# B's keys and values in 32 KB runs, and four heads finished together, in a two-cache attention decode kernel

## The chip, the cores and the metric

The kernel runs on one core of a Trainium2 chip. The metric is the device time of one execution in microseconds (us). A "fast" run is an undisturbed one. Engines: PE multiplies matrices (PEld is its loading of weights), DVE is the vector engine, ACT the scalar engine, POOL does next to nothing here, SP issues the DMAs.

## The reference

Two independent attention decode steps for one token, their outputs side by side. A attends to all 16384 keys of each of 32 heads, B only to the last 4096 keys of each of 32 heads.

```python
def _A_ref(x, k_cache, v_cache, wq, wo):       # x [1,1,512], caches [1,32,16384,128]
    q = (x @ wq).reshape(1, 1, 32, 128).transpose(0, 2, 1, 3)
    # ... (k, v are the caches themselves: rep is 1)
    scores = jnp.einsum("bhqd,bhkd->bhqk", q, k) * (128 ** -0.5)
    p = _softmax(scores, axis=-1)
    o = jnp.einsum("bhqk,bhkd->bhqd", p, v)
    return o.transpose(0, 2, 1, 3).reshape(1, 1, 4096) @ wo
# _B_ref: the same with k_cache[:, :, Sk - W:, :] and v_cache[:, :, Sk - W:, :], W = 4096
return jnp.concatenate([a, b], axis=-1)        # [1,1,1024], bfloat16
```

Every key and value is used once. The kernel has to read 352.3 MB.

## The kernel before

A *unit* is one head of A or four heads of B: 128 partitions x 128 keys of keys (4 MB) and the same of values. Key tiles and value tiles have two buffers each. A *chunk* is 64 keys on each partition, so a unit has two chunks. After every four A heads comes one B unit; a B unit is also the last of all.

For each chunk DVE multiplies the keys by the query (a tile `prod`), adds the two halves of the head dimension (`half`), PE sums on with an identity matrix (`red`), DVE ends the sum (`sc`), ACT takes the exponential (`p`), and PE multiplies `p` by the values into an accumulator: for every four keys on a partition a matmul with 4 stationary columns, on one of four column tiles (rows 0, 32, 64, 96).

How B lies in memory is the point of the change. Before, each B head covers all 128 partitions with 32 keys each, so a partition's piece of a head is 32 x 128 x 2 bytes = 8 KB. The four heads lie one behind the other in the tile, so a chunk needs two heads:

```python
def _load_kv(nc, cx, unit, which, cut_last=1):
    # ... (tile of 128 partitions x 128 keys x 128, view of the cache)
    L = st.W // P                                  # A: 128 keys a partition, B: 32
    for i, h in enumerate(unit.heads):
        src = view[h].rearrange("(p l) d -> p l d", p=P)
        cuts = cut_last if i == n - 1 else 1
        w = L // cuts
        for c in range(cuts):
            cx.o(nc.sync.dma_start(
                out=t[:, i * L + c * w : i * L + (c + 1) * w, :],
                in_=src[:, c * w : (c + 1) * w, :],
            ))

def _mult(nc, cx, ch):                             # one multiply for each head in the chunk
    for k0, n, st, h, _, _ in ch.pieces:
        q = st.qall[:, h * DH : (h + 1) * DH]
        cx.o(nc.vector.tensor_tensor(
            out=ch.prod[:, k0 : k0 + n, :],
            in0=ch.unit.kt[:, ch.k0 + k0 : ch.k0 + k0 + n, :],
            in1=q.rearrange("p (o d) -> p o d", o=1).broadcast_to([P, n, DH]),
            op=ALU.mult,
        ))
```

Each head of A and B has its own accumulator and is finished alone: copy, fp32 fold to one row, division, output product.

```python
        cx.o(nc.tensor.matmul(                     # in _pv
            acc[r : r + 4, :],
            lhsT=ch.p[:, k : k + 4],
            rhs=ch.unit.vt[:, ch.k0 + k : ch.k0 + k + 4, :],
            start=(first and t < 4), stop=(last and t >= T - 4)))
    # ...
def _fin_fold(nc, cx, st, heads):
    # ... (sums of the exponentials into column DH)
        for e in range(4):
            cx.o(nc.tensor.matmul(
                f_ps[0:1, x, 0:DH],
                lhsT=cx.sel[:, e : e + 1],
                rhs=acc_sb[:, e * DH : (e + 1) * DH],
                start=False, stop=(e == 3), skip_group_check=True))
```

Loads are issued by SP in a fixed order (keys of unit i, then values of unit i-1) as buffers come free. At the end the last chunks go through without a further multiply:

```python
    _softmax(nc, cx, prev)
    waiting.append(prev)
    for ch in waiting:
        fin_pe()
        fin_dve()
        pv(ch)
    while fins:
        fin_pe()
        fin_dve()
```

The softmax here doesn't subtract the row's maximum and nothing guards it: scores larger than these inputs give would overflow.

## Time and profile before

839.10 us (median of 4 runs, 838.87 to 839.16). The profiled execution has a span of 837.5 us.

The page of the kernel before: span, busy time of the engines, the rate in 40 equal slices of the span, and packets.

```profile
span 837.5 us, 7159 instructions
PE 446.3 (53%) x3007; PEld 175.5 (21%) x3008; DVE 585.5 (70%) x331; ACT 98.6 (12%) x339; POOL 0.8 (0%) x8
...
GB/s 384 443 425 425 417 434 432 431 437 425 417 437 431 423 429 422 436 430 422 437 426 431 424 423 435 426 437 428 425 420 435 436 428 424 416 440 428 427 422 183
DMA packets 21508, 352.79 MB, mean 421 GB/s; under 512 B 2530, under 2 KB 2532, under 8 KB 4836
```

No engine is near full. After the first slice the rate is steady near 430 GB/s, with slices of 416 to 422, until the last one. Groups of instructions of the kernel before (busy us, mean ns of one, then the idle time before them and what ended most of it):

```profile
L146 DVE TENSOR_TENSOR prod<-kt,qallA 128x8192 bf16<-128x8192 bf16 x64 | 283.2, 4425 | 216.3 <-DMA kt<-in_A_k_cache_dram 216.2
...
L146 DVE TENSOR_TENSOR prod<-kt,qallB 128x4096 bf16<-128x4096 bf16 x32 | 72.3, 2289 | 1.7 <-DMA kt<-in_B_k_cache_dram 1.1
L235 PE MATMUL f_ps<-acc_sb,sel 128*1 128x128 f32 x512 | 64.4, 272 | 16.2 <-ACT acc_sb L220 16.2
```

DVE waits 216.2 us for keys of A but only 1.1 us for keys of B. The stretches of the kernel before (window, length, busy us of PE, PEld, DVE, ACT, POOL, then granted PE clock (1.00 is full), share of the DMA engines, GB/s):

```profile
300.00:400.00 100.00, 52.26 (x363) 20.37 (x362) 69.09 (x40) 10.90 (x40) 0.00 (x0) 0.74 1.01 429
...
828.00:830.00 2.00, 2.00 (x26) 0.93 (x23) 0.16 (x1) 1.22 (x4) 0.00 (x0) 1.00 0.02 6
```

In the middle the DMA engines are saturated (share 1.01). From 828 us on they have next to nothing left to do (0.02). The last packet of the values ends at 828.3 us. Their landing is counted here, and in every run below, from the moment at which the load's semaphore is complete in the trace: 828.75 us.

| what | before |
|---|---|
| time, median | 839.10 us |
| DMA share, 100 to 800 us | 1.01, 428 to 429 GB/s |
| packets of 32 KB / of 8 KB | 8320 of 1219 ns / 8064 of 314 ns (mean durations of the DMA records) |
| DVE, PE, ACT busy | 70%, 53%, 12% |
| last values landed, span's end | 828.75 us, 837.5 us |

What does the end hang on? The chain of waits of the kernel before from 762 us on (start, length, what):

```profile
762.20 27.05 DMA kt<-in_A_k_cache_dram
...
789.35 0.06 DVE prod L146
...
818.54 3.57 PE red L171 x8
...
835.00 0.57 ACT rowB L289
```

The last DMA on this chain is the keys of the last *A* head, at 789.3 us. After it the chain runs over DVE and PE to the end. The end is thus a chain of computation over four chunks; the landing of the last values is not on it. But it is close by. PE's timeline of the kernel before at that place:

```profile
828.80 0.62 PE L209 MATMUL acc_101<-vt,p_sb 128*4 128x512 bf16 x5
829.25 1.03 PE L278 MATMUL outA<-wo_t,oc 128*1 128x512 bf16 x4
```

No wait stands before these matmuls. The first of them that needs the last values starts at 829.04 us by the records, 0.3 us after the landing: the two paths to the end differ by no more than that.

### The profile page before, as it was taken

The numbers are of one execution on the slowest core, as the hardware profiler recorded it, in microseconds if no ns is written. First come the engines' busy times: TensorE is split into PE (matmuls) and PEld (weight loads), VectorE is DVE, ScalarE is ACT, GpSimd is POOL, SyncE is SP. The second block draws the span as 40 slices with busy tenths as digits, with TensorE's granted clock in tenths as the row PEclk, the third lists the DMA queues.
The fourth block names the chain that finished last, engine by engine and source line by source line (L and its number), as shares of the span: only waits on it lengthen the run. The fifth ranks groups of instructions, "written<-read, shape, count | busy, mean of one in ns | idle before, by whom it ended". The sixth has DMA issues, their size and how long they took to land.

```text
span 837.5 us, 7159 instructions
## 1 busy us (share of the span) xinstructions
PE 446.3 (53%) x3007; PEld 175.5 (21%) x3008; DVE 585.5 (70%) x331; ACT 98.6 (12%) x339; POOL 0.8 (0%) x8
## 2 busy tenths in 40 slices
PE   3456635555365543655555643456556545355567
PEld 1122212212122211221122211222122112121123
DVE  1892936779577793677867685666947779377791
ACT  2002101001011010100111000111011001010012
POOL 0000000000000000000000000000000000000000
PEclk9578777777787686876778777787687787777678
DMA  9999999999999999999999999999999999999994
GB/s 384 443 425 425 417 434 432 431 437 425 417 437 431 423 429 422 436 430 422 437 426 431 424 423 435 426 437 428 425 420 435 436 428 424 416 440 428 427 422 183
DMA packets 21508, 352.79 MB, mean 421 GB/s; under 512 B 2530, under 2 KB 2532, under 8 KB 4836
## 3 DMA queue, kind: packets, MB, share of 16 engines
q1 hardware_dynamic: 21188, 352.33, 98.7%
q8 instruction: 23, 0.38, 0.2%
q14 instruction: 9, 0.07, 0.0%
q10 hardware_dynamic: 288, 0.00, 0.0%
HBM read 352.32 MB, written 0.00 MB: 421 GB/s over the span
## 4 chain that ended last, share of the span: by engine, by line
DMA 66%; DVE 21%; issue 9%; PE 3%; ACT 1%; SPq 0%; DVEq 0%; ACTq 0%
DMA kt<-in_A_k_cache_dram 53%; DVE prod L146 13%; DMA kt<-in_B_k_cache_dram 10%; DVE half L158 6%; DMA wq_t<-in_B_wq_dram 3%; DVE sc L183 2%; PE q_ps L101 1%; PE f_ps L235 1%; ACT qallB L108 0%; PE red L171 0%; PE acc_101 L209 0%; DVE recip L247 0%; SPq L136 0%; PE outB L278 0%; PE oc_ps L261 0%
## 5 line engine op out<-in xcount | busy, mean ns | idle before, releaser
L146 DVE TENSOR_TENSOR prod<-kt,qallA 128x8192 bf16<-128x8192 bf16 x64 | 283.2, 4425 | 216.3 <-DMA kt<-in_A_k_cache_dram 216.2
L171 PE MATMUL red<-half,ident 128*128 128x512 bf16 x640 | 236.1, 535 | 286.8 <-DVE half L158 286.8
L158 DVE TENSOR_TENSOR half<-prod 128x4096 bf16<-128x4096 bf16 x80 | 182.4, 2280 | 0.0
L171 PEld LDWEIGHTS <-ident 128*128 128x128 bf16 x640 | 78.0, 123 | 404.8 <-issue 376.8
L209 PE MATMUL acc_101<-vt,p_sb 128*4 128x512 bf16 x640 | 58.1, 485 | 59.9 <-DMA vt<-in_A_v_cache_dram 59.9
L146 DVE TENSOR_TENSOR prod<-kt,qallB 128x4096 bf16<-128x4096 bf16 x32 | 72.3, 2289 | 1.7 <-DMA kt<-in_B_k_cache_dram 1.1
L235 PE MATMUL f_ps<-acc_sb,sel 128*1 128x128 f32 x512 | 64.4, 272 | 16.2 <-ACT acc_sb L220 16.2
L187 ACT ACTIVATE p_sb<-sc 128x64 bf16<-128x64 f32 (+1 forms) x96 | 23.5, 245 | 355.3 <-DVE sc L183 355.3
L209 PEld LDWEIGHTS <-p_sb 128*4 128x4 bf16 x1280 | 27.8, 91 | 147.4 <-issue 137.0
L183 DVE TENSOR_REDUCE sc<-red 128x64 f32<-128x512 f32 x80 | 54.6, 683 | 3.7 <-PE red L171 3.7
L209 PE MATMUL acc_103<-vt,p_sb 128*4 128x512 bf16 x640 | 53.1, 448 | 6.0 <-DMA vt<-in_A_v_cache_dram 6.0
L235 PEld LDWEIGHTS f_ps<-acc_sb,sel 128*1 128x1 f32 x512 | 38.2, 83 | 29.2 <-ACT acc_sb L220 18.7
L220 ACT COPY acc_sb<-acc_103 128x512 f32<-128x512 f32 x32 | 18.7, 586 | 140.0 <-PE acc_103 L209 83.1
L220 ACT COPY acc_sb<-acc_101 128x512 f32<-128x512 f32 x32 | 18.8, 588 | 127.6 <-PE acc_101 L209 86.6
L250 ACT ACTIVATE orow<-f_ps,recip 1x128 bf16<-1x128 f32 x64 | 21.2, 354 | 86.4 <-DVE recip L247 86.4
L187 ACT ACTIVATION_READ_ACCUMULATOR p_sb<-sc 128x1 f32 x96 | 18.0, 188 | 0.0
L101 PE MATMUL q_ps<-wq_t,xbA 128*128 128x512 bf16 x32 | 9.3, 462 | 13.2 <-DMA wq_t<-in_A_wq_dram 13.2
L261 PEld LDWEIGHTS <-orow 1*32 1x32 bf16 x256 | 10.0, 110 | 27.7 <-issue 21.4
L261 PE MATMUL oc_ps<-one,orow 1*32 1x1 bf16 x256 | 14.1, 171 | 0.7 <-ACT orow L250 0.7
L229 PE MATMUL f_ps<-ones_col,cs 128*1 128x1 f32 x192 | 14.1, 165 | 0.0
L229 PEld LDWEIGHTS f_ps<-ones_col,cs 128*1 128x1 f32 x192 | 11.5, 85 | 11.7 <-issue 4.5
L247 DVE RECIPROCAL recip<-f_ps 1x1 f32<-1x1 f32 (+1 forms) x48 | 7.2, 150 | 8.2 <-PE f_ps L235 8.2
(25 smaller groups left out, 54.4 us busy)
## 6 DMA issues: line engine op xcount, KB each, us to landing
kt<-in_A_k_cache_dram SPq DMA_DIRECT2D x32, 4096.0 KB, 27.3
vt<-in_A_v_cache_dram SPq DMA_DIRECT2D x31, 4096.0 KB, 31.7
kt<-in_B_k_cache_dram SPq DMA_DIRECT2D x32, 1024.0 KB, 24.0
vt<-in_B_v_cache_dram SPq DMA_DIRECT2D x31, 1024.0 KB, 28.2
wq_t<-in_A_wq_dram SPq DMA_DIRECT2D x1, 4096.0 KB, 12.3
wq_t<-in_B_wq_dram SPq DMA_DIRECT2D x1, 4096.0 KB, 24.1
wo_t<-in_A_wo_dram SPq DMA_DIRECT2D x4, 1024.0 KB, 29.2
wo_t<-in_B_wo_dram SPq DMA_DIRECT2D x4, 1024.0 KB, 30.5
```

Source lines behind the costliest of these rows:

```text
L101: cx.o(nc.tensor.matmul(q_ps[:, :], lhsT=st.xb[:, c, :], rhs=st.wq_t[:, c, j * 512 : (j + 1) * 512], start=(c == 0), stop=(c == KC - 1),))
L146: cx.o(nc.vector.tensor_tensor(out=ch.prod[:, k0 : k0 + n, :], in0=ch.unit.kt[:, ch.k0 + k0 : ch.k0 + k0 + n, :], in1=q.rearrange("p (o d) ...
L158: cx.o(nc.vector.tensor_tensor(out=ch.half[:, :, :], in0=ch.prod[:, :, 0 : DH // 2], in1=ch.prod[:, :, DH // 2 : DH], op=ALU.add,))
L171: cx.o(nc.tensor.matmul(ch.red[:, :, :], lhsT=cx.ident[:, :], rhs=ch.half[:, :, b * W : (b + 1) * W], start=(b == 0), stop=(b == nb - 1),))
L183: cx.o(nc.vector.tensor_reduce(out=sc[:, :], in_=ch.red[:, :, :], axis=AX.X, op=ALU.add))
L187: cx.o(nc.scalar.activation(out=ch.p[:, k0 : k0 + n], in_=sc[:, k0 : k0 + n], func=ACT.Exp, scale=SCALE, accum_out=ch.cs[:, i : i + 1],))
L209: cx.o(nc.tensor.matmul(acc[r : r + 4, :], lhsT=ch.p[:, k : k + 4], rhs=ch.unit.vt[:, ch.k0 + k : ch.k0 + k + 4, :], start=(first and t < ...
L220: cx.o(nc.scalar.copy(st.acc_sb[h][:, :], acc[:, :]))
L229: cx.o(nc.tensor.matmul(f_ps[0:1, x, DH : DH + 1], lhsT=col, rhs=cx.ones_col[:, 0:1], start=(x == 0 and i == 0), stop=(i == len(cs) - 1), ...
L235: cx.o(nc.tensor.matmul(f_ps[0:1, x, 0:DH], lhsT=cx.sel[:, e : e + 1], rhs=acc_sb[:, e * DH : (e + 1) * DH], start=False, stop=(e == 3), s ...
L250: cx.o(nc.scalar.activation(out=orow[:, :], in_=f_ps[0:1, x, 0:DH], func=ACT.Copy, scale=recip[0:1, x : x + 1]))
L261: cx.o(nc.tensor.matmul(st.oc_ps[32 * hp : 32 * hp + 32, j : j + 1], lhsT=orow_j[:, j, :], rhs=cx.one[0:1, 0:1], start=True, stop=True,))
```

## The change

The intent: B's loads in long runs like A's, and far fewer small instructions to finish heads.

- B's head g of a unit goes on the partitions g, g+4, g+8, ...: 32 partitions with 128 keys each, 32 KB a partition. A chunk then holds keys of all four heads, and one multiply serves them: partition p of `qallB` holds the query of head p%4.
- Four heads share one accumulator, 16 rows to a column tile. `p` has zeros in the columns of the other heads. For A the tiles are zeroed once; for B each chunk has four exponentials with a bias of 0 or -1000 (`off`), which makes zeros on the other heads' partitions.
- Sums, fold, division and transposes are done for four heads at once.
- At the end: the last values come as a half and two quarters of the keys, four DMAs each; the last accumulator copy and the output row are split between ACT and DVE.

```diff
-def _load_kv(nc, cx, unit, which, cut_last=1):
+def _load_kv(nc, cx, unit, which, cuts=(2 * U,)):
...
-    L = st.W // P
     n = len(unit.heads)
-    for i, h in enumerate(unit.heads):
-        src = view[h].rearrange("(p l) d -> p l d", p=P)
-        cuts = cut_last if i == n - 1 else 1
-        w = L // cuts
-        for c in range(cuts):
-            cx.o(nc.sync.dma_start(
-                out=t[:, i * L + c * w : i * L + (c + 1) * w, :],
-                in_=src[:, c * w : (c + 1) * w, :],
-            ))
+    k = 0
+    for w in cuts:
+        for g, h in enumerate(unit.heads):
+            src = view[h].rearrange("(p l) d -> p l d", p=P // n)
+            cx.o(nc.sync.dma_start(out=t[g:P:n, k : k + w, :], in_=src[:, k : k + w, :]))
+        k += w
...
 def _softmax(nc, cx, ch):
...
+    for h in u.heads:
+        g = h % G
         cx.o(nc.scalar.activation(
-            out=ch.p[:, k0 : k0 + n],
-            in_=sc[:, k0 : k0 + n],
+            out=ch.p[:, :, g, :],
+            in_=sc[:, :].rearrange("p (t e) -> p t e", e=4),
             func=ACT.Exp,
             scale=SCALE,
-            accum_out=ch.cs[:, i : i + 1],
+            bias=0.0 if len(u.heads) == 1 else cx.off[:, g : g + 1],
+            accum_out=gr.cs[:, ch.i, g : g + 1],
         ))
...
         cx.o(nc.tensor.matmul(
-            acc[r : r + 4, :],
-            lhsT=ch.p[:, k : k + 4],
-            rhs=ch.unit.vt[:, ch.k0 + k : ch.k0 + k + 4, :],
+            gr.acc[r : r + 4 * G, :],
+            lhsT=ch.p[:, t, :, :],
+            rhs=u.vt[:, k : k + 4, :],
...
     if last:
-        st.acc_sb[h] = cx.accs_pool.tile([P, 4 * DH], F32, tag="accs", name="acc_sb")
-        cx.o(nc.scalar.copy(st.acc_sb[h][:, :], acc[:, :]))
+        final = gr.i == gr.st.H // G - 1 and gr.st.name == "B"
+        gr.acc_sb = []
+        for x in range(2):
+            t = cx.accs_pool.tile([P, 2 * DH], F32, tag=f"accs{x}", name="acc_sb")
+            copy = nc.vector.tensor_copy if final and x == 1 else nc.scalar.copy
+            cx.o(copy(t[:, :], gr.acc[:, x * 2 * DH : (x + 1) * 2 * DH]))
...
+    for e in range(4):
+        cx.o(nc.tensor.matmul(
+            gr.f_ps[:, 0:DH],
+            lhsT=cx.sel[:, e, :],
+            rhs=gr.acc_sb[e // 2][:, (e % 2) * DH : (e % 2 + 1) * DH],
+            start=False, stop=(e == 3), skip_group_check=True,
+        ))
...
-        cx.o(nc.scalar.copy(row[0:1, :], st.out_ps[0:1, :]))
+        n = st.DN // 2
+        cx.o(nc.scalar.copy(row[0:1, 0:n], st.out_ps[0:1, 0:n]))
+        cx.o(nc.vector.tensor_copy(row[0:1, n:], st.out_ps[0:1, n:]))
...
+    cuts = {n - 1: (U, U), n: (U, U // 2, U // 2)}
...
             ld.add("kt", lambda u=u: _load_kv(nc, cx, u, "k"))
...
-            ld.add("vt", lambda u=units[i - 1], c=(2 if i >= n - 1 else 1): _load_kv(nc, cx, u, "v", c))
+            ld.add("vt", lambda u=units[i - 1], c=cuts.get(i, (2 * U,)): _load_kv(nc, cx, u, "v", c))
```

## The prediction

> **What bounds it now.** The DMA engines. In the table of stretches the DMA share is 1.00 to 1.01 and the rate 428 to 429 GB/s in every 100 us stretch from 100 to 800 us; the page gives 352.3 MB read at a mean of 421 GB/s over the span of 837.5 us. DVE is 70% busy, PE 53%, ACT 12%. The chain of waits is 66% DMA, mostly the keys of A. Only the ends are not DMA-bound: the first 10 us (331 GB/s) and what follows about 825 us. In the timeline PE is busy without a break from 825 to 830 us (p.v of the last B heads mixed with fp32 folds of single heads), and finishing runs to 835.6 us.
>
> **What the change does.**
>
> 1. Packets. In the DMA records a packet of 32 KB takes 1219 ns on average (26.9 GB/s an engine), one of 8 KB 314 ns (26.1 GB/s). 8064 packets have 8 KB, nearly all of B's keys and values. On 16 engines they take 158.3 us; the same bytes in 32 KB packets take 153.6 us. That is 4.7 us off the saturated resource, so all of it should come off the span.
>
> 2. Fewer and wider finishes. The 512 fp32 folds (64.4 us of PE) become 64 and the 64 accumulator copies (587 ns each) 32 half-size ones. B's multiplies go from two of 2289 ns to one of about 4425 ns a chunk: 2.5 us of DVE in all. B's exponentials become four masked ones a chunk. Nearly all of this lies under DMA and is worth nothing, except at the end.
>
> 3. Tail. The last B values now come as a half and two quarters of each partition, for all four heads at once, finished in one fold. From the landing of the last values I estimate, with durations of the trace: 16 p.v matmuls partly done before (1 us), copy on two engines (0.4), A's output product (1.0), fold (0.8), reciprocal, row (0.6), 16 tiny transposing matmuls (1.0), cast (0.2), output product (1.0), row (0.4), store (about 2): 8 to 9 us, against about 10 to 11 us now. Worth 2 to 2.5 us.
>
> Sum: 839.1 - 4.7 - 2.3 = about 832 us. DMA bounds it still: 352.3 MB at 430 GB/s is 819 us plus start and tail, so 2% (822 us) is hardly reachable.
>
> **Risk.** Each B DMA now writes 32 partitions, every fourth one. The Trainium skill ("DMA: Bandwidth & Descriptors", The descriptor swizzle) says that in a 128-partition transfer each engine writes one port, four adjacent partitions and four more 32 further on; with a step of 4 each engine would then get two rows on its own port. No trace of this kernel shows how a 32-partition DMA is dealt out. If two engines meet on one port, B's 154 us could double. I give this about 6%.
>
> **Prediction.** 832 us, 80% range 827 to 837 us. Faster by over 2%: 4%; within 2%: 90%; slower by over 2%: 6%.
>
> **What the profile would show if right.** Packets 21508 to about 15500; the rate no longer dipping to 415-420 GB/s in slices; DMA share still 1.0; 32 KB packets still near 1219 ns; DVE about 582 us; PE down some 60 us with no gain from it; last landing of values about 4 to 5 us earlier, and 8 to 9 us from there to the end. **Wrong if:** B's packets are slower than A's (ports), DMA share falls below 1 in the middle (buffers of values freed later), or the tail is bound by the compute chain from the last keys rather than by the values' landing; then the tail gain vanishes.

## The result, and the profile after

836.09 us (median of 4 runs, 835.15 to 836.64) against 839.10: 0.9963 of the time before, 95% interval 0.9946 to 0.9981. A ratio is the mean time of one kernel's fast runs over that of the other's fast runs of the same rounds, so it is not quite the ratio of the medians that are quoted. The kernel is 3.0 us faster where 7.1 us were predicted. The time lies in the predicted range of 827 to 837 us, near its upper end; 4.1 us of the foreseen gain are missing.

The page of the kernel after, the same lines:

```profile
span 833.4 us, 6067 instructions
PE 409.5 (49%) x2496; PEld 140.3 (17%) x2496; DVE 586.0 (70%) x301; ACT 68.8 (8%) x316; POOL 2.8 (0%) x16
...
GB/s 379 450 425 428 416 440 429 431 436 433 431 429 429 428 431 430 434 429 436 427 433 427 427 434 429 433 429 432 429 430 433 430 428 427 434 431 431 433 422 186
DMA packets 15599, 352.71 MB, mean 423 GB/s; under 512 B 2642, under 2 KB 2644, under 8 KB 4692
```

The packets fell as foreseen, and from the sixth slice on the rate no longer dips below 427 GB/s until the last two. The profiled execution took 835.15 us, the fastest of the four. Its groups:

```profile
L164 DVE TENSOR_TENSOR prod<-kt,qallA 128x8192 bf16<-128x8192 bf16 x64 | 283.3, 4426 | 168.7 <-DMA kt<-in_A_k_cache_dram 168.0
...
L164 DVE TENSOR_TENSOR prod<-kt,qallB 128x8192 bf16<-128x8192 bf16 x16 | 70.8, 4426 | 51.9 <-DMA kt<-in_B_k_cache_dram 51.6
...
L265 PE MATMUL f_ps<-acc_sb,sel 128*4 128x128 f32 x128 | 16.6, 272 | 3.7 <-ACT acc_sb L251 3.7
```

The folds fell from 64.4 to 16.6 us. But DVE's wait for B's keys rose from 1.1 to 51.6 us, eight waits, one in each B unit. DVE's whole wait for keys hardly changed: 216.2 + 1.1 = 217.3 us before, 168.0 + 51.6 = 219.6 us after. In the middle this is a shift of idle time and costs nothing, as the stretches of the kernel after show:

```profile
300.00:400.00 100.00, 49.78 (x301) 16.37 (x300) 72.46 (x34) 7.67 (x38) 0.00 (x0) 0.70 1.00 430
...
820.00:822.00 2.00, 2.00 (x12) 0.78 (x15) 0.01 (x1) 0.00 (x0) 0.00 (x0) 1.00 0.93 344
```

The DMA share stays at 1.00. In the last unit it is otherwise. DVE's timeline of the kernel before (start, length, engine, line, operation), at the first multiply of the last B unit:

```profile
801.55 2.28 DVE L158 TENSOR_TENSOR half<-prod 128x4096 bf16<-128x4096 bf16 x1
803.86 4.49 DVE L146 TENSOR_TENSOR prod<-kt,qallB 128x4096 bf16<-128x4096 bf16 x2
```

and of the kernel after at the same place:

```profile
798.19 2.28 DVE L176 TENSOR_TENSOR half<-prod 128x4096 bf16<-128x4096 bf16 x1
805.46 4.42 DVE L164 TENSOR_TENSOR prod<-kt,qallB 128x8192 bf16<-128x8192 bf16 x1 [4.99 <-DMA kt<-in_B_k_cache_dram]
```

DVE was ready 3.4 us earlier than before (798.19 against 801.55), but waited 4.99 us for the last B keys and began its last unit 1.6 us later than before. The multiply of a chunk now needs all four heads' loads; before, it needed two. The chain of waits of the kernel after shows what the end hangs on:

```profile
780.07 25.26 DMA kt<-in_B_k_cache_dram
...
820.00 1.89 PE red L189 x8
821.88 1.00 PE acc_128 L236 x16
...
830.98 0.41 DVE rowB L319
```

The last DMA on the chain is now the last B unit's *keys* at 805.3 us. The last values land at 825.07 us, 3.7 us earlier than before, and 8.3 us before the end.

One more thing is to be seen at the end, in the timeline of ACT and of DVE of the kernel after:

```profile
826.60 0.37 ACT L251 COPY acc_sb<-acc_126 128x256 f32<-128x256 f32 x1 [1.43 <-PE acc_126 L236]
827.00 0.42 DVE L251 COPY acc_sb<-acc_126 128x256 f32<-128x256 f32 x1 [1.26 <-ACT acc_sb L251]
```

The two halves of the copy, which should have run side by side, ran one after the other: DVE waited for ACT. Together they take 0.82 us from 826.60 to 827.42, where a whole copy by ACT takes 0.59 us. (PE works on A's output product meanwhile, until 827.34 us in the chain of waits, so this copy is not on the chain here.) The output row shows the same order: ACT at 830.58, DVE at 830.98 us, and this one is on the chain.

### The profile page after: what moved, and what is told of

Read it like the earlier page. It is cut to its first block, busy times and chain, and to the rows that moved or that the text cites. A ratio compares the mean times of both kernels' runs of the same rounds, so it can differ in the third digit from the quotient of the medians.

```text
span 833.4 us, 6067 instructions
## 1 busy us (share of the span) xinstructions
PE 409.5 (49%) x2496; PEld 140.3 (17%) x2496; DVE 586.0 (70%) x301; ACT 68.8 (8%) x316; POOL 2.8 (0%) x16
## 4 chain that ended last, share of the span: by engine, by line
DMA 67%; DVE 20%; issue 10%; PE 1%; SPq 1%; ACT 0%; DVEq 0%; ACTq 0%
DMA kt<-in_A_k_cache_dram 55%; DVE prod L164 12%; DMA kt<-in_B_k_cache_dram 12%; DVE half L176 6%; DVE sc L206 2%; SPq L156 1%; PE acc_126 L236 0%; PE red L189 0%; PE f_ps L265 0%; PE outB L306 0%; PE acc_128 L236 0%; PE outA L306 0%; DVE recip L275 0%; DVEq L164 0%; PE oc_ps L287 0%
## 5 line engine op out<-in xcount | busy, mean ns | idle before, releaser
L189 PE MATMUL red<-half,ident 128*128 128x512 bf16 x640 | 255.5, 572 | 390.0 <-DVE half L176 390.0
L164 DVE TENSOR_TENSOR prod<-kt,qallA 128x8192 bf16<-128x8192 bf16 x64 | 283.3, 4426 | 168.7 <-DMA kt<-in_A_k_cache_dram 168.0
L189 PEld LDWEIGHTS <-ident 128*128 128x128 bf16 x640 | 82.9, 130 | 538.1 <-issue 512.5
L164 DVE TENSOR_TENSOR prod<-kt,qallB 128x8192 bf16<-128x8192 bf16 x16 | 70.8, 4426 | 51.9 <-DMA kt<-in_B_k_cache_dram 51.6
L213 ACT ACTIVATE p_sb<-sc,off 128x64 bf16<-128x64 f32 x64 | 21.5, 337 | 99.9 <-DVE sc L206 99.9
L236 PE MATMUL acc_126<-vt,p_sb 128*16 128x512 bf16 x256 | 20.3, 440 | 0.0
L265 PE MATMUL f_ps<-acc_sb,sel 128*4 128x128 f32 x128 | 16.6, 272 | 3.7 <-ACT acc_sb L251 3.7
L236 PE MATMUL acc_128<-vt,pA_122 128*16 128x512 bf16 x128 | 12.1, 518 | 5.3 <-DMA vt<-in_A_v_cache_dram 5.3
L236 PE MATMUL acc_128<-vt,pA_118 128*16 128x512 bf16 x128 | 11.1, 480 | 5.7 <-DMA vt<-in_A_v_cache_dram 5.7
L236 PE MATMUL acc_128<-vt,pA_110 128*16 128x512 bf16 x128 | 12.0, 514 | 0.0
L213 ACT ACTIVATION_READ_ACCUMULATOR p_sb<-sc,off 128x1 f32 x64 | 12.0, 187 | 0.0
L236 PE MATMUL acc_128<-vt,pA_114 128*16 128x512 bf16 x128 | 11.5, 494 | 0.0
L236 PE MATMUL acc_128<-vt,pA_120 128*16 128x512 bf16 x128 | 11.3, 489 | 0.0
L265 PEld LDWEIGHTS f_ps<-acc_sb,sel 128*4 128x4 f32 x128 | 9.9, 86 | 6.6 <-ACT acc_sb L251 4.5
L213 ACT ACTIVATE pA_124<-sc 128x64 bf16<-128x64 f32 x8 | 2.1, 256 | 106.6 <-DVE sc L206 106.6
L236 PE MATMUL acc_128<-vt,pA_116 128*16 128x512 bf16 x128 | 10.6, 462 | 0.0
L236 PE MATMUL acc_128<-vt,pA_112 128*16 128x512 bf16 x128 | 10.5, 460 | 0.0
L236 PE MATMUL acc_128<-vt,pA_124 128*16 128x512 bf16 x128 | 10.0, 442 | 0.0
L213 ACT ACTIVATE pA_116<-sc 128x64 bf16<-128x64 f32 x8 | 2.0, 256 | 90.6 <-DVE sc L206 90.6
```

Of the source, the lines that this page charges most:

```text
L164: cx.o(nc.vector.tensor_tensor(out=ch.prod[:, :, :], in0=u.kt[:, ch.k0 : ch.k0 + U, :], in1=q.rearrange("p (o d) -> p o d", o=1).broadcast ...
L189: cx.o(nc.tensor.matmul(ch.red[:, :, :], lhsT=cx.ident[:, :], rhs=ch.half[:, :, b * W : (b + 1) * W], start=(b == 0), stop=(b == nb - 1),))
L213: cx.o(nc.scalar.activation(out=ch.p[:, :, g, :], in_=sc[:, :].rearrange("p (t e) -> p t e", e=4), func=ACT.Exp, scale=SCALE, bias=0.0 if ...
L236: cx.o(nc.tensor.matmul(gr.acc[r : r + 4 * G, :], lhsT=ch.p[:, t, :, :], rhs=u.vt[:, k : k + 4, :], start=(first and t < 4), stop=(last an ...
L265: cx.o(nc.tensor.matmul(gr.f_ps[:, 0:DH], lhsT=cx.sel[:, e, :], rhs=gr.acc_sb[e // 2][:, (e % 2) * DH : (e % 2 + 1) * DH], start=False, st ...
```

## The experiments

Theory T: the longer packets gave all of the gain, though less than the 4.7 us predicted, and the cheaper ending gave nothing, because the chain from the last B keys holds the end. Rivals: the new partition layout costs DMA time (ports); the extra finishing work was not hidden before, so the gain comes from there; the new small last DMAs cost what was gained.

| run | what it is | median us (range) | before | ratio (95%) |
|---|---|---|---|---|
| e1_repeat | after, unchanged | 837.12 (835.69 to 838.14) | 839.04 | 0.9972 (0.9958 to 0.9986) |
| e2_pad8k | after with 8 KB packets for B | 839.68 (838.28 to 840.34) | 839.04 | 0.9999 (0.9986 to 1.0013) |
| e3_klast | after, last B keys in two halves | 834.84 (834.64 to 836.28) | 839.04 | 0.9956 (0.9942 to 0.9969) |
| e4_contig | after, a B head on 32 adjacent partitions | 1141.46 (1123.79 to 1157.94) | 839.04 | 1.3491 (1.34 to 1.3581) |
| e5_refold | after, folds done 8 times | 837.51 (836.73 to 838.49) | 839.10 | 0.9981 (0.9968 to 0.9993) |
| e6_klast_vhalves | e3 with last values in halves | 835.34 (834.82 to 836.79) | 839.10 | 0.9958 (0.9946 to 0.9971) |
| e7_klast_fin | e3 with a shorter finish | 834.42 (834.18 to 835.38) | 839.10 | 0.9946 (0.9933 to 0.9958) |
| e8_klast_fin_vhalves | e7 and e6 together | 834.93 (834.64 to 835.99) | 839.10 | 0.9951 (0.9938 to 0.9965) |
| e9_pad8k_klast | e2 and e3 together | 840.62 (839.13 to 841.61) | 839.16 | 1.0016 (1.0003 to 1.0030) |
| e10_before_rev | before, last four key loads in reverse order | 843.97 (842.28 to 844.85) | 839.16 | 1.0054 (1.0041 to 1.0066) |
| e11_pad8k_k3 | e2, last B keys as a half and two quarters | 839.23 (837.73 to 839.33) | 839.35 | 0.9991 (0.9978 to 1.0005) |
| e12_k3 | its partner with 32 KB packets | 835.88 (834.98 to 835.95) | 839.35 | 0.9956 (0.9944 to 0.9969) |

Each median is one of five runs, e4's of four. Every result was correct.

### e1_repeat: the changed kernel again

No edit. It gives the spread.

> The changed kernel once more, unchanged. Its four runs so far are 835.15, 835.59, 836.64 and 836.58 us, and only the fastest was profiled. This run shows whether a second profile has the same end. If the spread of 1.5 us sits in the end (last landing of values to the end of the span, 8.6 us in the first profile), DMA up to 800 us will be at the same place in both profiles within 0.3 us; if it sits in the DMA stream, the point where 300 MB had landed (698.6 us after the first packet) will move instead.

837.12 us, and a spread of 2.45 us, where the nine runs of the kernel before spread over 0.89 us. All nine runs of the changed kernel lie between 835.15 and 838.14, with a median of 836.64. The two profiles of it (835.15 and 838.14 us) tell where the spread comes from. In both, the first 300 MB are in at the same time (698.6 and 698.9 us after the first packet; worked out from the DMA records). They part at the end. A stretch and PE's timeline of e1_repeat:

```profile
820.00:822.00 2.00, 1.54 (x4) 0.55 (x4) 0.41 (x1) 0.00 (x0) 0.00 (x0) 0.50 0.91 340
```

```profile
820.46 3.57 PE L189 MATMUL red<-half,ident 128*128 128x512 bf16 x8 [2.96 <-DVE half L176]
823.96 1.88 PE L236 MATMUL acc<-vt,pA 128*16 128x512 bf16 x16
```

The same eight matmuls took 3.57 us here and 1.89 us in the first profile (the chain above), the next sixteen 1.88 and 1.04 us. The granted PE clock is 0.50 here and was 1.00 there. The Trainium skill ("TensorE: Matmul & The Clock Gate", What's actually happening) describes two states, half and full clock, set by how busy PE has been in a free-running window of some 3.4 us. These two profiles agree: their clock records hold 0.5 and 1.0 alone. That the phase of such a window decides between them is not shown by any run here. Near the end of the chain a change of this state is worth about 2.5 us, so single runs of the changed kernel can't be compared to less than that. In the kernel before, the same eight matmuls took 3.57 us too (its chain above).

### e2_pad8k: only the packets undone

Everything of the change stays, but a B tile has 32 bytes of padding after every 32 keys, so that a partition's run is cut into 8 KB packets again. (DVE multiplies in two halves then, as before the change.)

```diff
+PAD = 16
...
+            if n == 1:
+                cx.o(nc.sync.dma_start(out=t[:, k : k + w, :], in_=src[:, k : k + w, :]))
+            else:
+                b = 32 * DH + PAD
+                cx.o(nc.sync.dma_start(
+                    out=flat[g:P:n, k // 32 * b : (k + w) // 32 * b].rearrange("p (b x) -> p b x", x=b)[:, :, 0 : 32 * DH],
+                    in_=src[:, k : k + w, :].rearrange("p (b k) d -> p b (k d)", k=32),
+                ))
```

> The changed kernel with B's keys and values cut into 8 KB packets again (the tile of a B unit has 32 bytes of padding after every 32 keys), everything else as in the change but two half multiplies a chunk. Theory 1 (packets: each 8 KB packet costs more of the saturated DMA engines than a quarter of a 32 KB one): about 3.5 to 4.7 us slower than the changed kernel, that is 839 to 841 us, with B's packets at about 314 ns. Rival (the gain of the change came from the finishing and the tail, the packets gave nothing): within 0.7 us of the changed kernel.

839.68 us: 2.6 us over e1_repeat (2.3 us in the means), and nothing below the kernel before (0.9999). So the packets are worth about 2.3 to 2.6 us here (five runs each: a 95% interval of about 0.9 to 3.6 us, which leaves out 4.7), and the rest of the change, wider folds, shorter ending and all, is worth nothing as it stands. The expectation of 3.5 to 4.7 us was too high. The kernel still waited for the last B keys, as DVE's timeline of e2_pad8k shows:

```profile
808.76 4.49 DVE L189 TENSOR_TENSOR prod<-kt,qallB 128x4096 bf16<-128x4096 bf16 x2 [5.19 <-DMA kt<-in_B_k_cache_dram]
```

The DMA records say the same without the noise of the end: the first 300 MB were in 698.9 us after the first packet in e1_repeat and 700.8 us after it in e2_pad8k.

Why 2.6 and not 4.7? The prediction added up the durations of packet records. Take instead 4 us stretches of the trace in which over 99.5% of the bytes came in packets of one size, spread each packet's bytes evenly over its record, and count bytes (means over all such stretches):

| packets in the stretch | GB/s | DMA share by records |
|---|---|---|
| 32 KB, all three kernels | 431.5 to 431.7 | 1.003 |
| 8 KB, kernel before | 421.7 | 1.014 |
| 8 KB, e2_pad8k | 423.4 | 1.013 |

A share above 1 says that records of packets overlap a little, those of 8 KB by about 1% more than those of 32 KB. Their durations count some time twice, and their sum overstates their cost. From the rates, B's 66.06 MB (8064 x 8192 bytes) cost 66.06 MB x (1/421.7 - 1/431.6) = 3.6 us more in 8 KB packets, or 3.0 us with 423.4 GB/s. That is an estimate from the trace, and it lies between what is measured here and what was predicted.

### e3_klast: the last B keys in two halves

```diff
-            ld.add("kt", lambda u=u: _load_kv(nc, cx, u, "k"))
+            ld.add("kt", lambda u=u, c=((U, U) if i == n - 1 else (2 * U,)): _load_kv(nc, cx, u, "k", c))
```

Each of the four heads' loads of the last B unit becomes two, first halves first, so the first chunk needs only 2 MB of 4.

> The changed kernel with only the last B unit's keys loaded in two halves of 64 keys a partition, so that the first of its two chunks can start when half of the keys have landed. Theory (the tail gain was eaten because the multiply of the last B unit now waits for all four heads' keys: DVE idle 4.99 us at 805 us, which the kernel before did not have): the wait of about 5 us before that multiply goes, the last chunk's products are ready about 5 us earlier, and the end is then bound by the landing of the last values, 0.6 to 1.5 us earlier than now. Rival (the end is bound by the last values already): no change within 0.4 us.

834.84 us, 2.3 us below e1_repeat (1.8 us in the means). DVE's and PE's timeline of e3_klast:

```profile
800.87 4.42 DVE L164 TENSOR_TENSOR prod<-kt,qallB 128x8192 bf16<-128x8192 bf16 x1 [0.15 <-DMA kt<-in_B_k_cache_dram]
...
825.32 0.61 PE L236 MATMUL acc<-vt,p_sb 128*16 128x512 bf16 x8 [1.77 <-DMA vt<-in_B_v_cache_dram]
```

The wait before the multiply fell from 4.99 to 0.15 us, and the last p.v matmuls now wait for the values. The end of the chain of waits of e3_klast holds the DMA of B's values until 825.28 us:

```profile
820.36 4.92 DMA vt<-in_B_v_cache_dram
825.32 0.61 PE acc L236 x8
```

Only 2.3 of the 4.6 us by which the multiply began earlier came through, because the values' landing is then the next bound. The end after that landing is 7.7 us. What the wait had cost depends on the clock in the chain behind it: the span of e3_klast is 3.5 us shorter than that of e1_repeat (clock 0.50 at 820 us), but only 0.5 us shorter than that of the first profile (clock 1.00 there). The 2.3 us are a mixture of such runs; the interval of the means is about 0.5 to 3.1 us.

### e4_contig: 32 adjacent partitions

A B head on the partitions 32g to 32g+31, in place of every fourth; the query's layout and `off` follow.

```diff
-            cx.o(nc.sync.dma_start(out=t[g:P:n, k : k + w, :], in_=src[:, k : k + w, :]))
+            cx.o(nc.sync.dma_start(out=t[g * (P // n) : (g + 1) * (P // n), k : k + w, :], in_=src[:, k : k + w, :]))
```

> The changed kernel with the four heads of a B unit on 32 adjacent partitions each instead of on every fourth one; packets stay 32 KB. If the ports of the SBUF side matter[...], B's packets take up to twice 1218 ns and the time rises by something between 20 and 150 us. Rival (the step of 4 is only a convenience, four queued DMAs even it out): within 2 us of the changed kernel and B's packets at 1218 ns.

The two runs counted as fast took 1123.79 and 1140.40 us; the two others, 1142.52 and 1157.94, count as slow, though here it seems to be this kernel's own spread. The ratio from the fast runs is 1.3491; 20 to 150 us more had been expected, and it is about 290. Two lines of its page (the profile is of the run of 1157.94 us):

```profile
GB/s 399 434 431 254 365 317 432 309 339 255 429 385 236 291 258 290 367 239 304 245 342 363 226 327 204 342 370 244 312 224 317 390 246 326 205 328 352 230 210 65
...
L164 DVE TENSOR_TENSOR prod<-kt,qallB 128x8192 bf16<-128x8192 bf16 x16 | 70.8, 4426 | 201.6 <-DMA kt<-in_B_k_cache_dram 201.3
```

The rate falls to 204 to 260 GB/s again and again, and the 32 KB packets took 1561 ns on average (median 1218, the slowest hundredth over 3560). The Trainium skill ("SBUF — State Buffer", Door 1: The DMA port swizzle) gives 8 of 16 ports for the partitions 0 to 31, and 189 GB/s for a transfer of 1 MiB to them; the slices agree in kind. So the step of four is no detail: with it, loads of 32 partitions ran as fast as those of 128. The prediction's 6% risk was real for another layout and did not come about in this one: with the step of four, packets of 32 KB took 1218 ns, before the change 1219. The fast runs are some 293 us longer than the kernel before, nearly twice the 156 us that B's 67.1 MB need at 430 GB/s. Whether A's packets, queued behind, are slowed too was not separated.

### e5_refold: the folds done eight times

Every fold but the last of each problem is repeated eight times, which puts PE at 493.1 us of busy time, above the 446.3 of the kernel before.

```diff
+    for _ in range(1 if gr.i == gr.st.H // G - 1 else 8):
...
```

> The changed kernel with every fold but the two last ones done eight times over (the same sums, restarted each time, so the result stays right): about 392 more fp32 folds in the middle of the run, near the 448 that the change took away, some 50 to 60 us more of PE. Theory (the finishing work was under the DMA, so taking it away was worth nothing except at the end): within 0.6 us of the changed kernel. Rival (PE's time, or the later release of the buffers of values, cost something): slower by 1 us or more, with the DMA share below 1.00 in the middle.

837.51 us, 0.4 us above e1_repeat, within the spread. It was run at another time. The page and a stretch of e5_refold:

```profile
PE 493.1 (59%) x3672; PEld 214.3 (26%) x3672; DVE 586.1 (70%) x301; ACT 68.8 (8%) x316; POOL 2.8 (0%) x16
...
300.00:400.00 100.00, 59.35 (x470) 26.67 (x468) 71.86 (x34) 7.68 (x38) 0.00 (x0) 0.77 1.00 430
```

The DMA share in the middle stays at 1.00 to 1.01. So PE's finishing work was hidden under the DMAs, and saving it gave nothing there. The rival that finishing cost time in the middle falls, as far as PE's folds go; the copies by ACT and the transposing matmuls were not put back.

### e6, e7 and e8: what the end is made of

e6 gives e3_klast the last values as two halves, so four DMAs fewer at the end:

```diff
-    cuts = {n - 1: (U, U), n: (U, U // 2, U // 2)}
+    cuts = {n - 1: (U, U), n: (U, U)}
```

> The previous best (last B keys in two halves) with the last B values in two halves (8 DMAs of 16 KB packets) instead of a half and two quarters (12 DMAs, 8 KB packets at the end that took 338 to 349 ns against 311 elsewhere, DMA share 0.9 in the last 8 us). If the small last DMAs slow the stream: last landing 0.5 to 1 us earlier, which pays for the 8 more p.v matmuls left after it (0.5 us): -0.5 to 0 us. If the end of the stream is ragged because the 16 engines are not at the same place: same landing, +0.5 us.

835.34 us, 0.5 us above e3. The last values landed at 825.53 us instead of 825.28. The small last DMAs are thus not what slows the end. Only the shape differs: by the DMA records the share stays at 1.01 until 819 us in e6 and then falls, to 0.70 at 820 us, while in e3 it is at 0.85 to 0.93 from 817 us on. Why it falls in either stays open.

e7 gives e3_klast whole copies by ACT of the accumulator and the row in place of the split ones, and does A's output product before the last p.v matmuls, while PE waits for values:

```diff
-        gr.acc_sb = []
-        for x in range(2):
-            t = cx.accs_pool.tile([P, 2 * DH], F32, tag=f"accs{x}", name="acc_sb")
-            copy = nc.vector.tensor_copy if final and x == 1 else nc.scalar.copy
-            cx.o(copy(t[:, :], gr.acc[:, x * 2 * DH : (x + 1) * 2 * DH]))
-            gr.acc_sb.append(t)
+        gr.acc_sb = cx.accs_pool.tile([P, 4 * DH], F32, tag="accs", name="acc_sb")
+        cx.o(nc.scalar.copy(gr.acc_sb[:, :], gr.acc[:, :]))
...
         fin_dve()
+        if ch is prev:
+            fin_pe()
         pv(ch)
```

> The last B keys in two halves, and a shorter end: one ACT copy of the accumulator and of the output row (0.59 and 0.57 us) in place of a copy split between ACT and DVE, which the trace shows one after the other (0.37 + 0.42 us), and A's last output product (1.0 us of PE) before the last p.v instead of after it. Expected 0.3 to 0.8 us below the run with only the keys in halves (834.84), end after the last landing 7.1 us against 7.7. If the split copies did help: slower by 0.2 to 0.5 us.

834.42 us, the best of all: 0.9946 of the kernel before. The timelines of PE and ACT of e7_klast_fin:

```profile
825.05 0.61 PE L236 MATMUL acc<-vt,p_sb 128*16 128x512 bf16 x8 [1.19 <-DMA vt<-in_B_v_cache_dram]
825.76 0.59 ACT L247 COPY acc_sb<-acc 128x512 f32<-128x512 f32 x1 [1.72 <-PE acc L236]
```

The whole copy takes 0.59 us, against 0.82 us of the two halves. The end from the landing of the values is 7.4 us, against 7.7 in e3_klast. The gain over e3, 0.4 us of medians, is no more than the spread; the two profiles show 0.2 us of it in the end. They were run at other times.

e8 is both together.

> Both together: last keys in halves, last values in two halves, shorter end. Expected the sum of the two single effects, 833.8 to 834.8 us.

834.93 us, just above the expected range and again 0.5 us above the kernel with the half and two quarters. Smaller pieces at the very end pay a little, or nothing; they do not harm.

### e10_before_rev: the same wait, put into the kernel before

In the kernel before, the last B unit's four key loads are issued in reverse order of the heads, so its first multiply has to wait for the last of them, as in the kernel after. The number of loads, packets and bytes is the same.

```diff
-    for i, h in enumerate(unit.heads):
+    order = list(enumerate(unit.heads))
+    if which == "k" and n > 1 and unit.heads[-1] == st.H - 1:
+        order.reverse()
+    for i, h in order:
```

> The kernel before with one thing changed: the four loads of the last B unit's keys are issued in reverse order of the heads, so that its first multiply (head 0) waits for the last of the four to land, as the changed kernel's does. In the profile of before these four land from about 801.7 to 807.1 us and the multiply starts at 803.9. Theory (the end of the kernel before is a chain of DVE and PE work from this multiply on): about 3.3 us slower, 842 us, with a new wait of about 3 us of that multiply for B's keys. Rival (the end is set by the landing of the last values): within 0.5 us of before.

843.97 us, 4.8 us above the kernel before (1.0054). DVE's timeline of e10_before_rev:

```profile
809.06 4.49 DVE L149 TENSOR_TENSOR prod<-kt,qallB 128x4096 bf16<-128x4096 bf16 x2 [5.18 <-DMA kt<-in_B_k_cache_dram]
```

The wait of 5.18 us costs the old kernel nearly its whole length. (3.3 us had been expected, from a last landing of the keys at 807.1 us; the last of the four landed at 809.0.) This shows from the other side what the chain of waits of the kernel before said: its end was a chain of computation from the keys, with no room in it.

### e9, e11 and e12: the packets and the wait apart

e9 was to be e2 and e3 together: 8 KB packets, and no wait for the last keys.

> The kernel with 8 KB packets (839.68) with the last B keys in two halves. This is what the shared finishing and the new tail are worth without the packets and without the new wait. Theory (the finishing is worth about 2 us at the end, and the wait for the whole of the last B keys took it back): about 837.3 us, 1.5 to 2.5 us below the kernel with 8 KB packets and about 2 us below the kernel before. Rival (the gain from halving the last keys belongs to the large packets only): 839.0 or more.

840.62 us, and the aim was missed. In the built program the first multiply waited for all eight key loads (the trace shows waits for eight semaphores), and it waited 5.35 us. Why is not shown: its destinations have gaps, but so have those of e11. The run tells nothing of what it was made for.

e11 has the last B keys as a half and two quarters. There the built program waits for the first half only. e12 is the same with 32 KB packets:

```diff
-            ld.add("kt", lambda u=u: _load_kv(nc, cx, u, "k"))
+            ld.add("kt", lambda u=u, c=((U, U // 2, U // 2) if i == n - 1 else (2 * U,)): _load_kv(nc, cx, u, "k", c))
```

> The run before of this kind failed in its aim: with gaps in the destination the program made the first multiply of the last B unit wait for all eight key loads, so the wait of 5 us stayed. Here the last B keys come as a half and two quarters, and the built program waits for the first half only. 8 KB packets otherwise. Theory (shared finishing and tail are worth about 2 us once the wait is gone): 837 to 838 us, against 839.68 with the wait; the multiply no longer waits 5 us at about 809 us. Rival (the finishing is worth nothing at the end either): 839.0 or more with the wait gone.

> The partner of the run before it with 32 KB packets: the changed kernel with the last B keys as a half and two quarters. Expected as with two halves, 834.6 to 835.6 us. The difference of the two is what the packets are worth when the end is bound by the landing of the last values: 2.5 to 3.7 us from the rates measured in stretches of one packet size.

e11 took 839.23 us, e12 835.88: 3.35 us between them (3.1 us in the means, interval about 2.1 to 4.0), when the end hangs on the values' landing and not on the keys' wait. Not all of this is the packets. In the two profiles the last landing is 2.05 us apart (828.23 and 826.18 us) and the end after it 1.6 us longer in e11, at a lower PE clock.

Against the kernel before, e11 is only 0.1 us faster in the medians (0.5 us in the means). So the shorter finish, with the wait gone and the packets as before, still gives almost nothing: 837 to 838 us had been expected, and the rival's 839.0 or more came. One reason was seen above: in the kernel before the values' landing was only 0.3 us off the chain, so taking the keys' wait away could not bring the end far forward while the values landed as late as before. PE's timeline of e11_pad8k_k3 shows another:

```profile
828.37 0.72 PE L261 MATMUL acc<-vt,p_sb 128*16 128x512 bf16 x8 [1.96 <-DMA vt<-in_B_v_cache_dram]
828.85 1.91 PE L331 MATMUL outA<-wo_t,oc 128*1 128x512 bf16 x4
```

and the same lines of e12_k3:

```profile
826.31 0.61 PE L236 MATMUL acc<-vt,p_sb 128*16 128x512 bf16 x8 [1.97 <-DMA vt<-in_B_v_cache_dram]
826.74 1.02 PE L306 MATMUL outA<-wo_t,oc 128*1 128x512 bf16 x4
```

In e11 the values landed at 828.23 us, half a microsecond before those of the kernel before; then the four matmuls of A's output product took 1.91 us instead of 1.02, and the fold 1.72 instead of 1.03, at a granted clock of 0.50. PE had been waiting just before. Three of e11's runs took 839.23 to 839.33 us and two 837.73 and 838.13; that the clock is what parts them is likely but was profiled in one of them only.

## Why the prediction was right or wrong

The predicted sum was 839.1 - 4.7 (packets) - 2.3 (tail) = 832 us. What the runs put in its place is about -2 to -3 for the packets and about 0 for the tail (e2_pad8k, which has all of the change but the packets, equals the kernel before).

1. **What bounds the kernel: right.** DMA share 1.00 to 1.01 and 428 to 431 GB/s in every stretch of the middle, before and after. e5_refold, with more PE work than the kernel before, changed nothing there.
2. **Packets: the mechanism right, the size off.** The step was "8064 packets have 8 KB ... On 16 engines they take 158.3 us; the same bytes in 32 KB packets take 153.6 us. That is 4.7 us off the saturated resource". The term measured 2.3 to 2.6 us (e2 against e1) and 3.1 to 3.35 us (e11 against e12, of which some 1.6 us in the profiles are the PE clock). The records of packets overlap, and the rates in stretches of one packet size, 421.7 to 423.4 against 431.6 GB/s, would have said 3.0 to 3.6.
3. **The layout's risk: rightly small.** Packets of 32 KB took 1218 ns with the step of four; the rule of the Trainium skill that the prediction cited led to the right expectation, though no trace here shows how the rows are dealt out. e4_contig shows that with adjacent partitions the time would have been 1.35 of that before.
4. **Finishing is hidden: right.** PE fell by 36.8 us, not by the 60 foreseen: the folds fell by 47.8 us, but the 640 reducing matmuls took 572 ns each instead of 535, at a lower granted clock (0.723 on average, before 0.761). Nothing of it mattered.
5. **DVE's busy time: wrong, without effect.** Some 582 us were foreseen, 586.0 measured, 585.5 before. The busy times of DVE's groups add up to 604.6 us before and 602.2 after, so the work did fall by about what was foreseen; but the sums exceed the busy time of the page, so records of neighbouring instructions overlap, and fewer instructions overlap less. It is the same trap as in point 2.
6. **Tail: the step that failed.** The prediction said "From the landing of the last values I estimate ... 8 to 9 us, against about 10 to 11 us now. Worth 2 to 2.5 us." This took the values' landing as the start of the end. In the kernel after it is not, and in the kernel before it was not alone, with the chain from the keys 0.3 us behind it. The chain of waits shows the end of the kernel before as computation from the last A keys on, and that of the kernel after as computation from the last *B keys* on. Putting four heads on every chunk made the first multiply of the last unit wait for all four heads' loads, 4.99 us. The wait is two of the four 1 MB loads long: 2.1 MB at 431.6 GB/s are 4.9 us, an estimate from the trace. e3_klast took this wait away and got 2.3 us. That this is the amount predicted for the tail is chance: it varies with the clock from 0.5 to 3.5 us in the profiles, and e11 got next to nothing. e10_before_rev put the wait into the old kernel and lost 4.8 us. The prediction had named this under "wrong if", as a tail "bound by the compute chain from the last keys", and gave it no weight in the sum. It could have been read beforehand from the unchanged line for the keys in the diff, the order of the four loads, and the chain of waits.
7. **Tail, its size.** The kernel before needs 8.8 us from the last landing, not 10 to 11. The kernel after needs 8.3 us in one profile and 11.0 us in another, where the PE clock was at 0.50 until 826 us. With the wait gone (e3_klast, clock 1.00) it needs 7.7 us. So even then the shorter ending is worth 1.1 us, half of the term. And the copy "on two engines (0.4)" took 0.82 us, as the two ran in turn.
8. **The last landing** came 3.7 us earlier, where 4 to 5 were foreseen; of this, 2.9 us were there when 300 MB were in (698.6 against 701.5 us after the first packet).

What stays open: what sets the granted PE clock at the end in each run, and so about 2.5 us of spread in the changed kernel; why the DMA share falls below 1 in the last microseconds of loading (in the kernel after, 13 of the 16 increments of the last load's semaphore come by 823.93 us and the other three at 825.07); and how e4's 293 us divide between B's packets and those behind them.

The best version is e7_klast_fin: the change, with the last B keys in halves, the last copies whole, and A's output product ahead of the last values. It takes 834.42 us, 0.54% below the kernel before by ratio.

## What to carry to other kernels

When loads are merged or spread over the partitions, ask what the first instruction on them must now wait for. In a saturated middle such a coarser dependency costs nothing, but in the last unit it lies on the chain; cut the last loads along the new grain (here one line for about 2 us). Before you cost an ending, follow the chain of waits back to the last DMA on it, and don't take the last landing for it. Cost a packet size by bytes over time in stretches of one size, not by the sum of packet durations. Where two paths end within a few tenths of a microsecond of each other, shortening the later one gives no more than those tenths.

## What the Trainium skill lacked or had wrong

- "DMA: Bandwidth & Descriptors", Specifications, puts the smallest transfer for line rate at 512 B. Packets of 8 KB ran at 421.7 to 423.4 GB/s and those of 32 KB at 431.6 in the same kernels, 2% apart, worth 2 to 3 us of 839. The page's fixed cost for each packet (Why small descriptors are slow) is worked out for 256 B only; it has no rate of packets of 8 or 32 KB.
- "DMA: Bandwidth & Descriptors", Where 436 GB/s comes from, says that for transfers from HBM the side of HBM (about 358 GB/s) binds. This core, the only one that the program uses, read at 428 to 431 GB/s in stretches of 100 us, near the 435 that the page gives for the fabric. The page's own table of single-core measurements has up to 425 GB/s; the sentence lacks that condition.
- "DMA: Bandwidth & Descriptors", The descriptor swizzle, tells of 128-partition transfers only. A transfer to 32 partitions with a step of four ran at full rate (1218 ns for 32 KB), and one to 32 adjacent partitions did not (1561 ns, the average of all 32 KB packets of that kernel, A's included).
- No page was found that says that records of packets can overlap, so that durations add up to more than the time: the share of the DMA engines came to 1.014 in stretches of 8 KB packets.
- "TensorE: Matmul & The Clock Gate" has the two clock states, and that the number of slow matmuls varies from run to run. What it doesn't say is how much a chain at the end of a kernel varies by it: the same eight matmuls took 1.89 us in one run and 3.57 us in another, where the runs of the kernel spread over 3 us.
